# Forgetting attention and FFN on one core: no unread matmuls among the early pairs, the first weight piece behind the first scores, and two FFN quanta fewer beside each of the pairs 8 to 11

## The chip, the cores and the metric

The kernel runs on one core of one Trainium2 chip. Five engines work side by side and meet only at semaphores: TensorE (PE in the profile, its weight loads PEld), VectorE (DVE), ScalarE (ACT), GpSimd (POOL) and SyncE (SP), which here issues all the DMAs. The metric is the device time of the whole program in microseconds (us), lower is better. Three runs of the kernel before took 1208.0, 1208.28 and 1208.91 us; the median is 1208.28 us.

## The reference

Batch 8, 8 heads, sequence 576, head width 64. Attention has a decay that comes from the running sum of log f, and its output goes through a two-layer FFN with 4608 tokens, width 512 and inner width 2048, all in float32:

```python
scores = (1/sqrt(D)) * q @ k.T
cum    = cumsum(log(clip(f, 1e-4, 1)))
scores = where(causal, scores + cum[:, None] - cum[None, :], -1e9)
attn   = exp(scores - max) / (sum + 1e-9)
x      = (attn @ v) laid out as tokens x 512
out    = leaky_relu(x @ w_in, 0.01) @ w_out
```

## The kernel before, in words

The program is written in a fixed order and then reordered by a scheduler that knows the dependencies and its own estimate of each duration: an instruction may be placed ahead of others on its engine when its inputs are ready sooner. A step marked `keep_in_program_order` is pinned behind the step traced just before it on the same engine. Each engine then executes its own list strictly in order.

**Start and pairs.** For the first three batches (`NE = 3`) the first 256 query positions are done early and apart from the rest, two heads at a time: 4 pairs a batch, 12 pairs. In each pass of the loop at line 732, `early_load` fetches the next pair's q, k and v, `early_scores` computes the two row blocks of each head (matmuls `sce<-qk`, then `sce<-both`, which adds the decay; on VectorE the reduction at line 323 with the maximum; on ScalarE the exponential at line 327; then the normalisation, for the first four pairs on VectorE at line 336), `weights` prepares FFN weight pieces, `early_values` transposes and multiplies with v for the pair before, and `fill` issues FFN work. `early_scores` also issues `WARM[1]` matmuls on a tile of zeros after each row block of the first `WARM[2]` pairs. Nothing reads their result. `WARM[0]` more of them stand at the very start of the program.

**Weight pieces.** The FFN weights arrive in 16 pieces of 1 MB (`wraw`), fetched into two buffers, so piece n + 2 can be fetched when piece n is no longer read. `load_weight(n)` converts a piece: ScalarE at line 181 writes `wt`, VectorE shifts it at line 185 (pieces 0 to 4) or 187, ScalarE copies the high part at line 192, VectorE makes the low part (lines 194 and 195, or 206 to 211), and for pieces 0 to 4 TensorE sums it (`ws`), read back at line 204. `wt` has one buffer. For piece 0 the steps of lines 181 and 185 are pinned. `WQ` gives the number of pieces converted beside each pair: one for pairs 1 to 8, two for pairs 9 to 12. Before the loop, pieces 0 and 1 are fetched and piece 0 is converted.

**FFN.** Tokens go through in groups of 256. One block of FFN work for a group, 256 of the inner width, consists of four quanta: two of 12 matmuls `h` (128x256 each), then, for the block before, two of 6 matmuls `o` (128x512). Between them ScalarE applies the activation (`g`, line 654), and `gh` and `gl` split it into a rounded part and a remainder (lines 657 and 659; `gl` is made on VectorE beside the pairs and on POOL beside the heads). `fill(n)` adds n to a credit and issues as many quanta as it holds. `FQ` lists the quanta for each of the 12 pairs and for the pass behind them; three groups, 96 quanta, become ready in this part.

**Heads.** Then the other attention work follows, one head after another (64 tasks, batches in the order of `ORDER`): scores, transposes, values. Beside each head FFN quanta are issued: those ready and not used, `have`, are divided by the heads up to the end of the batch plus `SLACK`, an eighth of the share at each call:

```python
have = ready[0] // T * NQ - used[0]
left = min((e + 2 - t for e in ends if e + 1 >= t), default=1)
step = min(have / (left + SLACK), CAPS.get(t, MAXQ)) / 8
```

When the last head is done, the remaining quanta run one after another to the end.

Of the kernel before, what the change touches and what calls it, by code (L numbers as in the profile page):

```python
# [25 lines left out]
NE = 3  # L26
WQ = (1, 1, 1, 1, 1, 1, 1, 1, 2, 2, 2, 2)
ZE = (("z0", "z1", "z2", "z3"), ("e0", "e1", "e2", "e3"))
FQ = (0, 0, 0, 0, 4, 8, 8, 8, 8, 8, 8, 4, 2)
BUFS = dict(s1=2, m1=2, ost=2)  # L30
RAWS = ("ph", "pl")
WARM = (20, 2, 6)
SCALED = 4
SUMMED = 5
NEG = -1.0e30
# [5 lines left out]
def forgetting_attention_ffn(ctx, tc, qT, kT, v4, vr, f, w_in, w_out, out):  # L41
# [77 lines left out]
    def warm(n):  # L119

        ps = psum.tile([P, 512], F32, tag="h", name=f"warm_{len(warmed)}")
        warmed.append(n)
        for _ in range(n):
            matmul(ps, still[:, :P], still, start=True, stop=True)

    warm(WARM[0])
    eye = one.tile([P, P], F32, tag="part0", name="eye")
# [36 lines left out]
    def fetch_weight(n):  # L164
        raw = raws[n] = one.tile([P, 2, 4 * P, 2], I32, tag=RAWS[n % 2], name=f"wraw_{n}")
        for k, src in enumerate(wpieces[n][0]):
            nc.sync.dma_start(raw[:, k].rearrange("p w two -> p (w two)"), src)
# [47 lines left out]
    def weights(n):  # L215
        while len(loaded) < min(n, len(wpieces)):
            load_weight(len(loaded))
# [80 lines left out]
    def early_scores(b, g):  # L298
# [3 lines left out]
        for i in range(2):  # L302
# [14 lines left out]
            for o in range(2):  # L317
# [11 lines left out]
                )  # L329
            if b * HPB // 2 + g < WARM[2]:  # L330
                warm(WARM[1])
        nc.vector.tensor_scalar(sm, sm, 1.0e-9, None, op0=ALU.add)
# [47 lines left out]
    def fix_z():  # L380

        for i in range(NCH):
            z = fixed[f"z{i}"] = one.tile([P, (i + 1) * P], F32, tag=f"z{i}", name=f"fixed_z{i}")
            nc.gpsimd.memset(z if i == 0 else z[:, i * P + REST:], 0.0)
        fixed["vs"] = one.tile([P, 2, NCH, 2 * D], F32R, tag="vs", name="fixed_vs")

    def split(t):


        s, c0, c1 = tasks[t]  # L390
        h = state[t]
        a, n = c0 * P, S
        x = "ab"[t % 2]
        s1 = h["s1"] = one.tile([P, S], F32R, tag="s1", name=f"s1_{t}", bufs=2)
        m1 = h["m1"] = one.tile([P, S], F32R, tag="m1", name=f"m1_{t}", bufs=2)
        s2, m2 = h["s2"], h["m2"] = fixed["s2" + x], fixed["m2" + x]
        raw = h["raw"]
        for y, x in ((s1[:D, a:n], raw[:D, a:n]), (m1[D:, :n], raw[D:, :n])):
            last = nc.scalar.copy(y, x)  # L399
            if t < 2:  # L400
                tc.keep_in_program_order(last)
        for y in (s1, s2):
            nc.sync.dma_start(y[D:, a:n].bitcast(F32), s1[:D, a:n].bitcast(F32))
        nc.sync.dma_start(m1[:D, :n].bitcast(F32), m1[D:, :n].bitcast(F32))
        nc.sync.dma_start(s2[2:4, a:n].bitcast(F32), dec_q[s][:, a:n])
        nc.sync.dma_start(m2[:2, :n].bitcast(F32), dec_k[s][:, :n])
        minus(m2[D:, :n], raw[D:, :n], m1[D:, :n].bitcast(F32))
        minus(s1[:D, a:n], raw[:D, a:n], s1[:D, a:n].bitcast(F32))
# [291 lines left out]
    def fill(n):  # L700

        settle()
        credit[0] += n
        while credit[0] >= 1:
            credit[0] -= 1
            if not next(quanta, None):
                credit[0] = 0
                return
            used[0] += 1
# [18 lines left out]
    early_load(0, 0)  # L728
    for n in range(len(RAWS)):
        fetch_weight(n)  # L730
    weights(1)
    for x, (b, g) in enumerate(steps + [(NE, 0)]):
        if x + 1 < len(steps):
            early_load(*steps[x + 1])
# [15 lines left out]
        if x == len(steps):  # L750
            split(1)
        fill(FQ[x])
    fix_z()
# [72 lines left out]
```

## Time and profile before

| What | Value |
|---|---|
| Median of three runs | 1208.28 us (1208.0 to 1208.91) |
| Profiled execution, its own time | 1209.36 us |
| Span in the profile, first to last instruction | 1207.5 us |
| TensorE busy | 1194.9 us, 99% |
| TensorE weight loads busy | 1068.1 us, 88% |
| VectorE busy | 613.2 us, 51% |
| ScalarE busy | 633.2 us, 52% |
| GpSimd busy | 460.8 us, 38% |
| HBM read and written | 65.32 MB and 18.58 MB |
| First FFN matmul in the chain | 46.65 us |

How to read it. Busy time is an average over stages with different limits. Matmuls are pipelined and their ends are modelled, so a busy TensorE is not one at its peak. The chain of work that ended last is followed back from the last instruction, at each step to what released it. A timeline row gives the start and length in us, the engine and line, the operation, the tile written and the tiles read, the count, and in brackets the idle time before it with what ended it. A row of the table by stretch gives from : to, its length, then busy us (and count) of TensorE, weight loads, VectorE, ScalarE and GpSimd, then the granted TensorE clock, the DMA engines' share and GB/s.

### The profile page before, as it was taken

The numbers are of one execution on the slowest core, as the hardware profiler recorded it, in microseconds if no ns is written. First come the engines' busy times: TensorE is split into PE (matmuls) and PEld (weight loads), VectorE is DVE, ScalarE is ACT, GpSimd is POOL, SyncE is SP. The second block draws the span as 40 slices with busy tenths as digits, with TensorE's granted clock in tenths as the row PEclk, the third lists the DMA queues.
The fourth block names the chain that finished last, engine by engine and source line by source line (L and its number), as shares of the span: only waits on it lengthen the run. The fifth ranks groups of instructions, "written<-read, shape, count | busy, mean of one in ns | idle before, by whom it ended". The sixth has DMA issues, their size and how long they took to land.

```text
span 1207.5 us, 22521 instructions
## 1 busy us (share of the span) xinstructions
PE 1194.9 (99%) x7828; PEld 1068.1 (88%) x7828; DVE 613.2 (51%) x1697; ACT 633.2 (52%) x1622; POOL 460.8 (38%) x473
## 2 busy tenths in 40 slices
PE   9999999999999999999999999999999999999998
PEld 6678888888899999999999999999999999998997
DVE  6888365566655555464544445444443434553221
ACT  5887465666755565555554545455444445552111
POOL 2000255555455445454435354444354543531000
PEclk9999999999999999999999999999999999999999
DMA  6565233334343233323332223232233223311000
GB/s 202 175 204 177 78 99 101 99 111 118 102 137 82 82 99 101 99 72 97 87 96 79 80 66 101 65 100 59 69 85 93 58 71 81 80 58 52 13 18 19
DMA packets 82130, 110.57 MB, mean 92 GB/s; under 512 B 20640, under 2 KB 51728, under 8 KB 82016
## 3 DMA queue, kind: packets, MB, share of 16 engines
q1 hardware_dynamic: 82016, 109.12, 31.2%
q8 instruction: 63, 1.03, 0.4%
q14 instruction: 51, 0.42, 0.1%
HBM read 65.32 MB, written 18.58 MB: 69 GB/s over the span
## 4 chain that ended last, share of the span: by engine, by line
PE 95%; DVE 2%; ACT 1%; DMA 1%; issue 1%; POOL 0%; SPq 0%; DVEq 0%; ACTq 0%; POOLq 0%
PE h L111 34%; PE o L111 33%; PE tr L115 8%; PE av L111 8%; PE sc L111 7%; PE sce L111 2%; PE ave L111 1%; PE ws L111 1%; PE warm L111 1%; PE tre L115 1%; DVE fixed_z L437 1%; DMA wraw<-in_w_in 0%; ACT g L654 0%; DVE pl L489 0%; DVE gh L657 0%
## 5 line engine op out<-in xcount | busy, mean ns | idle before, releaser
L659 POOL TENSOR_TENSOR gl<-g,gh 128x512 fp32r<-128x512 f32 x113 | 148.8, 1317 | 275.1 <-DVE gh L657 270.1
L111 PE MATMUL o<-wout_h,gh 128*128 128x512 f32 x576 | 231.3, 402 | 0.0
L111 PE MATMUL o<-wout_l,gh 128*128 128x512 f32 x576 | 227.4, 395 | 0.0
L111 PE MATMUL o<-wout_h,gl 128*128 128x512 f32 x576 | 227.1, 395 | 0.0
L443 ACT ACTIVATE fixed_z<-fixed_z,max 128x192 f32<-128x192 f32 (+3 forms) x272 | 161.0, 592 | 101.4 <-DVE max L437 99.1
L111 PE MATMUL h<-xh,win_h 128*128 128x256 f32 x1152 | 206.2, 286 | 0.0
L487 ACT CAST ph<-tr 128x192 fp32r<-128x192 f32 (+3 forms) x360 | 126.7, 373 | 148.5 <-PE tr L115 99.2
L111 PE MATMUL h<-xh,win_l 128*128 128x256 f32 x1152 | 200.3, 283 | 0.0
L437 DVE CUSTOM_DVE_ANT_0 fixed_z<-sc,tri 128x192 f32<-128x192 f32 (+3 forms) x272 | 122.4, 451 | 151.3 <-PE sc L111 148.4
L654 ACT ACTIVATE g<-h 128x512 f32<-128x512 f32 x144 | 85.8, 596 | 216.1 <-PE h L111 211.0
L657 DVE CAST gh<-g 128x512 fp32r<-128x512 f32 x144 | 72.4, 503 | 217.6 <-ACT g L654 215.9
L489 DVE TENSOR_TENSOR pl<-tr,ph 128x384 fp32r<-128x384 f32 (+3 forms) x296 | 137.3, 467 | 80.7 <-ACT ph L487 79.5
L111 PEld LDWEIGHTS h<-xh,win_h 128*128 128x128 f32 x1152 | 170.8, 190 | 5.8 <-issue 0.5
L111 PEld LDWEIGHTS h<-xh,win_l 128*128 128x128 f32 x1152 | 164.8, 190 | 0.5 <-issue 0.2
L111 PE MATMUL h<-xs,win_h 128*128 128x256 f32 x1024 | 164.4, 283 | 0.0
L115 PE MATMUL tr<-ident_r,fixed_z 128*128 128x128 f32 x888 | 145.3, 273 | 3.4 <-DVE ph L494 1.7
L111 PEld LDWEIGHTS h<-xs,win_h 128*128 128x128 f32 x1024 | 141.0, 191 | 0.0
L115 PEld LDWEIGHTS tr<-ident_r,fixed_z 128*128 128x128 f32 x888 | 107.6, 140 | 25.2 <-ACT rb L566 5.2
L111 PEld LDWEIGHTS o<-wout_h,gl 128*128 128x128 f32 x576 | 108.2, 188 | 24.4 <-DVE maxe L323 0.3
L111 PEld LDWEIGHTS o<-wout_l,gh 128*128 128x128 f32 x576 | 108.7, 189 | 16.0 <-issue 0.5
L111 PEld LDWEIGHTS o<-wout_h,gh 128*128 128x128 f32 x576 | 108.9, 189 | 14.8
L154 POOL TENSOR_TENSOR fixed_m2a<-raw,m 64x576 fp32r<-64x576 f32 x32 | 46.6, 1458 | 195.4 <-ACT m L399 173.8
(130 smaller groups left out, 1753.2 us busy)
## 6 DMA issues: line engine op xcount, KB each, us to landing
raw<-in_kT SPq DMA_DIRECT2D x64, 144.0 KB
m<-m SPq DMA_DIRECT2D x64, 144.0 KB
wraw<-in_w_in SPq DMA_DIRECT2D x16, 512.0 KB
wraw<-in_w_out SPq DMA_DIRECT2D x16, 512.0 KB
fixed_vm<-in_v SPq DMA_DIRECT2D x64, 128.0 KB
xs<-xd SPq DMA_DIRECT2D x16, 512.0 KB
out<-ost SPq DMA_DIRECT2D x28, 256.0 KB
raw<-in_qT SPq DMA_DIRECT2D x40, 144.0 KB
```

The source lines that it names most:

```text
L111: nc.tensor.matmul(*args, **kw)
L115: nc.tensor.transpose(*args)
L154: nc.gpsimd.tensor_tensor(out, a, b, op=ALU.subtract)
L437: nc.vector.tensor_tensor_reduce(out=z[:, a:b], in0=ps[:m, :b - a], in1=tri[:m, at:at + b - a], scale=-SCALE, scalar=3.0e38 if x == 0 else ...
L443: nc.scalar.activation(z, z, AF.Exp, bias=h["max"][:m, last:last + 1], scale=-1.0, accum_out=fixed["sum" + "ab"[s // 2 % 2]][:m, i, s % 2: ...
L487: nc.scalar.copy(strided(ph, run), source(ps, run))
L489: nc.vector.tensor_tensor(strided(pl, run), source(ps, run), strided(ph, run).bitcast(F32), op=ALU.subtract)
L654: nc.scalar.activation(g, ph, AF.Prelu, alpha=0.01)
L657: nc.vector.tensor_copy(gh, g)
L659: eng.tensor_tensor(gl, g, gh.bitcast(F32), op=ALU.subtract)
```

## The change

Three constants and one call change. `WARM` keeps the 20 matmuls at the start and drops those among the pairs: after each of two row blocks of six pairs, two each, 24 in all. The call `weights(1)` ahead of the loop goes; piece 0 is then converted by the call `weights(sum(WQ[:x + 1]))` in the loop's first pass, behind `early_scores` of the first pair, and the two pinned steps of piece 0 follow that pair's steps on ScalarE and VectorE. The later passes convert the same pieces as before. In `FQ` the pairs 8 to 11, counted from 1, have 6 quanta each where they had 8; the eight quanta stay ready and are issued by the later calls of `fill`.

```diff
-FQ = (0, 0, 0, 0, 4, 8, 8, 8, 8, 8, 8, 4, 2)
+FQ = (0, 0, 0, 0, 4, 8, 8, 6, 6, 6, 6, 4, 2)
 BUFS = dict(s1=2, m1=2, ost=2)
 RAWS = ("ph", "pl")
-WARM = (20, 2, 6)
+WARM = (20, 0, 0)
...
     early_load(0, 0)
     for n in range(len(RAWS)):
         fetch_weight(n)
-    weights(1)
     for x, (b, g) in enumerate(steps + [(NE, 0)]):
```

## The prediction

> **What bounds the kernel now.** I read the page first: busy shares (its part 1) and the chain that ended last (part 4).
>
> ```profile
> PE 1194.9 (99%) x7828; PEld 1068.1 (88%) x7828; DVE 613.2 (51%) x1697; ACT 633.2 (52%) x1622; POOL 460.8 (38%) x473
> PE 95%; DVE 2%; ACT 1%; DMA 1%; issue 1%; POOL 0%; SPq 0%; DVEq 0%; ACTq 0%; POOLq 0%
> ```
>
> TensorE is busy 99% of the span and carries 95% of the chain. So the time is TensorE's work plus the short stretches in which it lacks work: work taken out counts, but only where nothing else then ends last. The table by stretch (us busy per engine) shows where another engine is close:
>
> ```profile
> 46.00:75.00 29.00, 29.00 (x194) 23.60 (x192) 27.73 (x59) 22.21 (x50) 0.00 (x0) 1.00 0.58 194
> 75.00:83.00 8.00, 8.00 (x49) 5.49 (x47) 5.99 (x18) 6.71 (x18) 0.00 (x0) 1.00 0.63 210
> 83.00:95.00 12.00, 12.00 (x78) 9.60 (x77) 10.58 (x23) 10.23 (x25) 0.00 (x0) 1.00 0.56 181
> 95.00:110.50 15.50, 15.46 (x100) 12.91 (x98) 12.47 (x25) 9.67 (x22) 0.00 (x0) 1.00 0.59 202
> 110.50:127.50 17.00, 16.20 (x99) 13.05 (x98) 11.84 (x24) 11.59 (x25) 3.06 (x2) 1.00 0.38 117
> ...
> 160.00:200.00 40.00, 39.16 (x263) 35.36 (x263) 23.99 (x63) 23.10 (x60) 23.25 (x26) 1.00 0.35 96
> 200.00:250.00 50.00, 49.40 (x335) 44.97 (x334) 28.69 (x91) 34.22 (x89) 24.42 (x27) 1.00 0.40 106
> 250.00:300.00 50.00, 47.99 (x324) 43.09 (x323) 30.91 (x97) 33.49 (x94) 28.10 (x30) 1.00 0.39 109
> 300.00:350.00 50.00, 48.81 (x329) 44.13 (x327) 31.36 (x94) 32.22 (x91) 24.13 (x24) 1.00 0.42 117
> 350.00:400.00 50.00, 50.00 (x340) 45.59 (x339) 27.86 (x81) 28.98 (x81) 26.62 (x26) 1.00 0.34 98
> ```
>
> The third busy number is VectorE. Beside the pairs it is nearly full (27.73 of 29.00 us from 46 to 75), and from 83 on it has 12% to 30% left. From 160 to 350 TensorE sits idle for 0.84 + 0.60 + 2.01 + 1.19 = 4.64 us, from 350 to 400 not at all. These are the two places that the moved FFN work leaves and enters.
>
> **Part 1: 24 matmuls go.** The first argument of `WARM` stays, so 20 of the 44 remain.
>
> ```profile
> L111 PE MATMUL warm<-still x44: 388/393/792, 1.5 to 56.2; 128*128 128x512 f32 x44
> ```
>
> ```profile
> 8.80 4.30 PE warm L111 x18
> ...
> 13.28 0.51 PE warm L111 x2
> ...
> 46.65 2.02 PE h L111 x17
> ...
> 54.61 0.47 PE warm L111 x2
> ...
> 56.15 0.47 PE warm L111 x2
> ```
>
> The chain charges 4.30 + 0.51 = 4.81 us to the 20 that were drawn ahead into the first scores, and 0.94 us to the other four. If TensorE had other work ready everywhere, the sum would be -5.75 us. It has not. The four at 54 to 57 stand where VectorE is 96% busy (27.73 of 29.00), so their ends are 0 and -0.94; I take -0.5, the middle, as both engines are near full there.
>
> For the 20, timeline rows (start, length) tell what stands behind them:
>
> ```profile
> 7.84 0.79 DVE L230 TENSOR_TENSOR both<-d,both 64x128 fp32r<-64x128 f32 x2
> ...
> 8.73 4.38 PE L111 MATMUL warm<-still 128*128 128x512 f32 x18
> 9.96 1.13 ACT L181 ACTIVATE wt<-wraw 128x1024 f32<-128x1024 f32 x1 [1.77 <-DMA wraw<-in_w_in]
> ...
> 12.95 0.34 PE L111 MATMUL sce<-both 128*128 128x128 f32 x2
> ...
> 13.32 0.29 DVE L323 CUSTOM_DVE_ANT_0 ze<-sce,tri 128x128 f32<-128x128 f32 x1 [4.68 <-PE sce L111]
> ...
> 13.71 0.40 ACT L327 ACTIVATE ze<-ze,maxe 128x128 f32<-128x128 f32 x1 [2.63 <-DVE maxe L323]
> ...
> 13.73 0.85 PE L111 MATMUL sce<-qk 64*128 64x256 f32 x4
> ...
> 13.75 0.69 DVE L185 TENSOR_SCALAR wt<-wt 128x1024 int32<-128x1024 int32 x1
> ...
> 15.20 1.23 DVE L195 SCALAR_TENSOR_TENSOR win_l<-wraw 128x1024 fp32r<-128x1024 uint32 x1
> ...
> 16.45 0.81 SPq L167 DMA_DIRECT2D wraw<-in_w_in  x2
> ...
> 18.28 0.41 DVE L323 CUSTOM_DVE_ANT_0 ze<-sce,tri 128x256 f32<-128x256 f32 x1
> ...
> 21.09 1.00 DVE L336 TENSOR_SCALAR ze<-ze,sume 128x128 f32<-128x128 f32 x4
> ```
>
> The decay rows `both` are ready at 7.84 + 0.79 = 8.63, but the matmul that adds them to the scores starts at 12.95, behind 18 unread matmuls; VectorE idles 4.68 us for it, and ScalarE 2.63 us. Without them that matmul follows at 8.73: everything of pair 0 begins 12.95 - 8.73 = 4.22 us earlier.
>
> **Part 2: piece 0 behind pair 0's scores.** The move issues no DMA and shifts no fetch: both fetches stay ahead of it in SP's queue. What moves is its first ScalarE step (L181), pinned behind the step traced before it, now the last exponential of pair 0; and its first VectorE step (L185), pinned behind the last of pair 0's four scalings (L336). So I lay out pair 0 from the rows: first reductions at 13.32 - 4.22 = 9.10, second score matmuls at 13.73 - 4.22 = 9.51 for 0.85, adding the decay for about 0.4, the wider reductions (0.41 each) at about 10.7 and 11.1, two exponentials to about 12.2, sum and reciprocal 0.35, scalings 1.00: end at about 13.5. L185 then starts at about 13.5 where it started at 13.75: piece 0 gains almost nothing (the low bound, 0.25 us), pair 0 the full 4.2 (the other bound). Between them: VectorE's stretch from 13.75 to 21.09 + 1.00 = 22.09 holds the two wide reductions (0.82), two small steps (0.35) and the scalings (1.00), about 2.2 us, that now lie ahead of piece 0; what remains ends 2.2 + 0.25, about 2.5 us, earlier. That value lies nearest to VectorE's rows, which are what ended the waits there, so I take -2.5 us of the 4.81; the other 2.3 us TensorE waits for piece 0 and the exponentials.
>
> Behind the late L181 and L185 stand the rest of piece 0 and the fetch of piece 2 (16.45, when L195 ends and its buffer is free). That fetch stays where it was and is what is late next:
>
> ```profile
> 18.00:20.00 2.00, 1.24 (x6) 0.93 (x7) 1.99 (x9) 1.89 (x7) 0.00 (x0) 1.00 0.96 389
> 20.00:21.00 1.00, 1.00 (x3) 0.25 (x3) 0.83 (x5) 1.00 (x3) 0.00 (x0) 1.00 0.42 168
> 21.00:22.00 1.00, 1.00 (x8) 0.66 (x8) 1.00 (x5) 0.55 (x4) 0.00 (x0) 1.00 0.00 0
> ```
>
> ```profile
> 23.53 1.14 ACT L181 ACTIVATE wt<-wraw 128x1024 f32<-128x1024 f32 x1
> ```
>
> The last two columns are the DMA engines' share and GB/s: they move nothing from 21 to 22, and ScalarE reads piece 2 at 23.53: at least 2.5 us of cover, just enough for the 2.5 us taken.
>
> **Part 3: eight quanta leave pairs 8 to 11.** Two columns of 12 `h` matmuls and two of 6 `o` matmuls make a block of four quanta; the chain's last full block:
>
> ```profile
> 1192.64 2.77 PE o L111 x12
> 1195.42 2.87 PE h L111 x24
> ```
>
> So a quantum is (2.77 + 2.87) / 4 = 1.41 us, eight are 11.3 us. This work is not saved: it must be done later, and it is free only where the pairs' stretch gets shorter by as much. From 75 to 127.5 us that leaves TensorE 52.5 - 11.3 = 41.2 us. VectorE has 5.99 + 10.58 + 12.47 + 11.84 = 40.9 us there, less two blocks' `gh` and `gl`:
>
> ```profile
> 100.09 0.43 DVE gh L657
> ...
> 101.64 0.68 DVE gl L659
> ```
>
> 2 x 1.11 = 2.2, so 38.7 us. At the 96% of the row 46 to 75 this takes 40.3 us and costs nothing; at the 88% of 83 to 95, 43.9 us, +2.7; at the 80% of 95 to 110.5, 48.1 us, +6.9. With less TensorE work beside it VectorE will wait less, so the value lies between the first two: +1.5 us. The quanta come back beside the first attention heads (96 ready quanta less the 58 used before, now 50, so 46 in place of 38; a head takes 9 calls of an eighth of that over 12, its remaining heads and slack: 8 / 12 x 9 / 8 = 0.75 more a head). The idle 4.64 us there is the most that this can win, nothing the least; I take a third, -1.5 us, since those waits come in links of the heads' own chain, not all of them where a quantum is put. `gl` of the two blocks passes to POOL, 38% busy.
>
> **Sum.** -2.5 - 0.5 + 1.5 - 1.5 = -3.0 us. The profiled execution took 1209.36 us (1.86 outside its span), 1.08 above the median of the three runs; against it 1206.4, against the median of 1208.28 it is 1205.3 us. A change under 0.2%, 2.4 us, can't be told from none here.
>
> **Rivals.**
> 1. *All of the 20 matmuls' time is won, and the stalls beside the heads too*: -4.2 - 0.9 + 0 - 3 = -8.1, 1200.2. For it: pair 0 does start 4.2 earlier. Against: piece 0 doesn't.
> 2. *The 20 were cover only*: piece 0, not pair 0, leads the start; -0.25 - 0.5, no net effect of the quanta: 1207.5, no change. For it: L185 moves 13.75 to 13.5 only. Against: VectorE has 4.68 us idle ahead of it.
> 3. *The pairs' stretch is held by the weight pieces*, VectorE at the 80% of 95 to 110.5: the eight quanta leave, the stretch shrinks by 4.4 and not 11.3. Then +6.9 in place of +1.5: +2.4, 1210.7, slower. It decides where VectorE's share falls below about 85% (38.7 / 0.85 = 45.5 us, +4.3, which eats up all the rest). For it: 110.5 to 127.5 shows 70%. Against: there TensorE, with eight quanta, was the one full.
> 4. *TensorE's clock drops in the thin start.* Matmul counts per 2 us show that the chip starts slow:
>
> ```profile
> 2.00:4.00 2.00, 2.00 (x6) 1.57 (x5) 1.00 0.77 223
> ...
> 6.00:8.00 2.00, 2.00 (x11) 1.61 (x9) 1.00 1.01 373
> ```
>
> Six unread matmuls before 4 us, eleven after 6, though the granted-clock column says 1.00 in both. From 8.73 to about 13.5 TensorE would have only about 2 of 4.8 us filled. If it went back to the slow rate until refilled, about 4.5 us (the slow stretch at the start) to 9 us of its work would take 11/6 as long: +4 to +7; with +4, 1209.3, no change. The Trainium skill, "TensorE: Matmul & The Clock Gate", Part 1, says that the clock falls after an idle window of about 3.4 us and rises after a busy one as long. The trace agrees with the rise; no gap that I lay out reaches an idle window, so by that rule the rival doesn't happen.
>
> **Chances.** The forecast 0.48, rival 1 0.12, rival 2 0.17, rival 3 0.13, rival 4 0.10. The forecast's own spread is about 3 us to either side: an eighth of it falls under 0.2%. Faster: 0.42 + 0.12 and 0.04 from rivals 2 and 4; slower: rival 3 and 0.02 of rival 4; the rest the same. The range goes from near rival 1 to rival 3: 1200.5 to 1210.5; the likeliest case alone is 1202.3 to 1208.3.
>
> **What would show it.** Right: 20 unread matmuls left; the decay matmul of pair 0 at about 8.8 and L185 at 13 to 14; the first `h` matmul, at 46.65 before, 2 to 3 us earlier; the pairs' end some 13 us earlier, the last full blocks at the old pace; less TensorE idle from 150 to 340. Wrong: piece 2's first step waiting for its DMA; TensorE idle beside pairs 8 to 11 with ScalarE waiting for a weight piece; matmul spacing near twice the old one between 10 and 20 us; the heads' idle time unchanged although each has more to fill it with.

## The result and the profile after

The changed kernel took 1216.27 us (median of five runs, 1215.22 to 1218.69), the kernel before, run beside it, 1208.28 (1207.43 to 1208.91): a ratio of 1.0070, interval 1.0055 to 1.0085. It is 8.0 us slower; the forecast was 3 us faster. The profiled execution took 1215.97 us, with a span of 1214.2. Among the runs below, two executions far out of line with the others of their kernel, 1910.39 us of the first experiment and 4068.62 us of the changed kernel with the old quanta, are left out of medians and ranges.

The page of the changed kernel, busy time and the chain by engine:

```profile
PE 1197.7 (99%) x7804; PEld 1067.9 (88%) x7804; DVE 620.2 (51%) x1696; ACT 632.6 (52%) x1622; POOL 461.9 (38%) x474
PE 92%; DVE 2%; ACT 2%; DMA 1%; issue 1%; POOL 1%; SPq 1%; ACTq 0%; POOLq 0%; DVEq 0%
```

TensorE runs 24 matmuls fewer and is busy 2.8 us longer, with 92% of the chain in place of 95%. Both point at a short stretch in which the chain leaves TensorE and its matmuls get longer. The chain of the first 60 us (start, length) shows where it leaves:

```profile
6.93 6.91 DMA qk<-in_kT
13.97 6.33 PE sce L111 x14
...
21.91 4.12 PE ws L111 x6
```

Until 13.84 the transfer of pair 1's k ends last, then scores are computed, and piece 0's products (`ws`) come only behind them. The timeline of the start (start, length, engine, line, count, and in brackets the idle time before with what ended it):

```profile
8.38 0.44 PE L111 MATMUL sce<-both 128*128 128x128 f32 x2
...
8.86 0.29 DVE L323 CUSTOM_DVE_ANT_0 ze<-sce,tri 128x128 f32<-128x128 f32 x1 [0.22 <-PE sce L111]
...
12.00 1.09 ACT L181 ACTIVATE wt<-wraw 128x1024 f32<-128x1024 f32 x1
...
13.97 0.76 PE L111 MATMUL sce<-qk 64*128 64x128 f32 x2 [3.41 <-DMA qk<-in_kT]
...
15.17 0.29 DVE L323 CUSTOM_DVE_ANT_0 ze<-sce,tri 128x128 f32<-128x128 f32 x1 [3.92 <-PE sce L111]
...
18.31 1.00 DVE L336 TENSOR_SCALAR ze<-ze,sume 128x128 f32<-128x128 f32 x4
...
19.22 0.69 DVE L185 TENSOR_SCALAR wt<-wt 128x1024 int32<-128x1024 int32 x1
```

Pair 0 starts as early as forecast. But between its last reduction and its scalings VectorE's list now holds reductions of pair 1 (at 15.17, after 3.92 us of waiting), and TensorE's list has all of pair 1's scores ahead of piece 0. Those scores wait 3.41 us for k, which was requested behind the 2 MB of the first two weight pieces. Piece 0's shift (L185) starts at 19.22, where it started at 13.75 before.

The table by stretch (from : to, length, busy us of TensorE, weight loads, VectorE, ScalarE and GpSimd, granted clock, DMA share, GB/s) shows the second thing:

```profile
0.00:10.00 10.00, 8.16 (x30) 6.12 (x30) 5.83 (x15) 5.07 (x11) 6.14 (x19) 1.00 0.70 220
10.00:20.00 10.00, 6.59 (x17) 3.93 (x16) 3.68 (x18) 3.81 (x13) 0.00 (x0) 0.60 0.39 137
20.00:30.00 10.00, 10.00 (x36) 5.60 (x36) 6.08 (x19) 4.75 (x10) 0.00 (x0) 0.71 0.27 88
```

A granted clock of 0.60 and 0.71 over 10 us each is (0.40 + 0.29) x 10 / 0.5 = 13.8 us at half clock. The trace's record of the clock has it as one stretch from 12.07 to 25.72, 13.65 us, which is four times 3.41 us, the shortest fall in these traces before the last 4 us of the program; 3.41 us at half clock is called a window below. The kernel before had 1.00 here throughout. All five runs of the changed kernel had a mean clock of 0.993 or 0.994; the 15 to 23 runs of before that stood beside each group of experiments nearly all had 1.0.

The heads, which were to take the eight moved quanta for nothing, give back nothing that their idle time shows:

```profile
160.00:200.00 40.00, 39.91 (x269) 36.26 (x268) 21.58 (x59) 21.45 (x56) 22.88 (x25) 1.00 0.33 91
200.00:250.00 50.00, 49.94 (x336) 45.03 (x335) 28.88 (x88) 30.36 (x83) 24.50 (x26) 1.00 0.39 111
250.00:300.00 50.00, 46.79 (x323) 42.67 (x324) 33.13 (x95) 33.78 (x95) 25.46 (x25) 1.00 0.38 108
300.00:350.00 50.00, 48.46 (x326) 43.81 (x325) 31.08 (x98) 34.36 (x95) 24.03 (x26) 1.00 0.39 107
```

TensorE is idle 0.09 + 0.06 + 3.21 + 1.54 = 4.90 us from 160 to 350, where it was 4.64. The small gaps before 250 are gone; a single one of 2.5 us at 270 has taken their place.

### The profile page after: what moved, and what is told of

It reads as the page before. It is cut to its first block, busy times and chain, and to the rows that moved or that the text cites. A ratio compares the mean times of both kernels' runs of the same rounds, so it can differ in the third digit from the quotient of the medians.

```text
span 1214.2 us, 22471 instructions
## 1 busy us (share of the span) xinstructions
PE 1197.7 (99%) x7804; PEld 1067.9 (88%) x7804; DVE 620.2 (51%) x1696; ACT 632.6 (52%) x1622; POOL 461.9 (38%) x474
## 4 chain that ended last, share of the span: by engine, by line
PE 92%; DVE 2%; ACT 2%; DMA 1%; issue 1%; POOL 1%; SPq 1%; ACTq 0%; POOLq 0%; DVEq 0%
PE h L111 33%; PE o L111 32%; PE tr L115 8%; PE av L111 8%; PE sc L111 7%; PE sce L111 2%; PE ws L111 1%; PE ave L111 1%; PE tre L115 1%; DMA qk<-in_kT 1%; DVE fixed_z L437 0%; DMA wraw<-in_w_out 0%; DVE pl L489 0%; DVE wraw L207 0%; DMA fixed_s2a<-s 0%
## 5 line engine op out<-in xcount | busy, mean ns | idle before, releaser
L659 POOL TENSOR_TENSOR gl<-g,gh 128x512 fp32r<-128x512 f32 x114 | 152.0, 1333 | 283.7 <-DVE gh L657 280.1
L657 DVE CAST gh<-g 128x512 fp32r<-128x512 f32 x144 | 75.4, 524 | 205.5 <-ACT g L654 204.1
L111 PE MATMUL sc<-m,s 128*128 128x288 f32 (+1 forms) x336 | 121.2, 365 | 0.5 <-DVE max L437 0.4
```

Source lines behind the costliest of these rows:

```text
L111: nc.tensor.matmul(*args, **kw)
L657: nc.vector.tensor_copy(gh, g)
L659: eng.tensor_tensor(gl, g, gh.bitcast(F32), op=ALU.subtract)
```

## The experiments

Times are medians; ratios are to the kernel before, run on the same chip. "Mean clock" is the granted clock over one execution. The first theory, A, was that pair 1's late transfer makes the gap and the gap drops the clock; B, that the thin start drops it with or without the gap; C, that the quanta cost.

### One part at a time

**Pair 1 fetched ahead of the weight pieces** (changed kernel; the lists of TensorE and VectorE stay):

```diff
     early_load(0, 0)
+    early_load(*steps[1])
     for n in range(len(RAWS)):
...
-        if x + 1 < len(steps):
+        if 1 < x + 1 < len(steps):
             early_load(*steps[x + 1])
```

> The changed kernel with pair 1's q, k and v fetched ahead of the two weight pieces; the order of TensorE's and VectorE's lists is that of the changed kernel. Theory A (pair 1's scores stand ahead of piece 0 in both lists and wait until 13.97 us for a transfer queued behind 2 MB of weights; the 3.4 us gap then halves TensorE's clock): the gap at 10.6 to 14.0 goes, L185 starts at 14 to 15 us and not at 19.22, the clock doesn't fall, and the kernel takes 1203 to 1207 us. Theory B (the start without unread matmuls is too thin for the clock, whatever is waited for): the clock still falls for some 10 us, 1211 us or more. Theory C (the eight FFN quanta are what costs): 1215 us or more, since they stay moved.

1214.01 us (1211.74 to 1215.14), ratio 1.0044, 1.0031 to 1.0057. The gap is gone and the shift starts at 15.6 instead of 19.2. The clock fell all the same:

```profile
10.00:14.00 4.00, 3.53 (x15) 2.25 (x15) 1.85 (x13) 3.03 (x10) 0.00 (x0) 0.99 0.95 366
14.00:20.00 6.00, 6.00 (x16) 3.67 (x16) 4.68 (x15) 3.61 (x11) 0.00 (x0) 0.50 0.25 67
```

TensorE's rows cover 3.53 of the 4 us before the fall, all of them small score matmuls, and the clock halves behind them. So A's second half fails: the gap is not needed. It costs more with the gap (four windows in place of two, from 13.90 on), but B is the better account of the clock in this run. C, 1215 or more, fell.

**The order alone** (kernel before without the call `weights(1)`; the 24 unread matmuls and the old quanta stay):

> The kernel before with piece 0 behind pair 0's scores alone; the 24 unread matmuls and the FFN quanta stay as before. Theory A: the unread matmuls cover the wait for pair 1, so the clock stays at 1.0, but piece 0 is still behind pair 1's scores in the lists, L185 starts at 17 to 19 us and the kernel takes 1210 to 1213 us. Theory B: with the unread matmuls in place nothing is lost, 1207 to 1209 us. Theory C: 1207 to 1209 us.

1215.51 us (1212.34 to 1215.96), ratio 1.0049, 1.0036 to 1.0061. Moving the call alone makes most of the loss; B and C, which had 1207 to 1209, fell. Two of its five executions had a clock of 1.0, and they took 1212.34 and 1212.76, in A's range: 3.5 to 4.0 us of loss with no fall of the clock at all. In the other three the clock fell although the unread matmuls were in place, which A did not have. In the profiled one it fell for two windows from 17.65 on, with no gap over 0.41 us in the 4 us before it, and the shift started at 20.3.

**The unread matmuls alone** (kernel before with `WARM = (20, 0, 0)`):

> The kernel before without the 24 unread matmuls among the pairs alone; piece 0 stays ahead of the loop, the quanta as before. Theory A: piece 0 is ahead of pair 1 in both lists, so no gap of 3 us; L185 at 11.2 to 12 us, clock at 1.0, 1203 to 1206 us. Theory B: the thin start lets the clock fall, 1209 to 1214 us. Theory C: as theory A.

1209.23 us (1206.99 to 1211.72, eleven runs), ratio 1.0006, 0.9998 to 1.0015. The three executions at clock 1.0 took 1206.99 to 1208.56, those below, 1208.22 to 1211.72. The shift starts at 10.6. A's 1203 to 1206 was missed; the median and the lower clocks are B's. At full clock the three lie 0.3 to 1.8 us under the median of before, whose own runs go from 1207.27 to 1210.34, so that a gain is not shown; in most executions the clock takes it back in any case.

**The quanta alone** (kernel before with the new `FQ`):

> The kernel before with the eight FFN quanta moved alone. Theories A and B: what the pairs' stretch loses the heads give back, 1206 to 1210 us. Theory C: 1213 us or more.

1212.89 us (1208.51 to 1214.70, ten runs), ratio 1.0029, 1.0018 to 1.0040. The two executions at clock 1.0 took 1208.51 and 1208.63, as before and as A and B had it. The others lost about 4, and the median lies between the ranges of A and B (to 1210) and of C (from 1213). The chain near the last weight pieces:

```profile
111.76 0.45 SPq L296
...
112.30 0.55 SPq L360
...
112.90 0.42 SPq L167
...
113.38 6.61 DMA wraw<-in_w_out
```

With less FFN work beside it the last weight fetch (L167) is reached behind other transfers in SP's queue, and ScalarE's step waits until 120.09. TensorE idles 2.34 us at 120.5, and the clock falls for a window:

```profile
120.00:127.00 7.00, 4.66 (x22) 3.14 (x21) 4.31 (x12) 4.60 (x11) 2.50 (x5) 0.76 0.12 34
```

### Filling the gap, nothing else

To part the clock from the order, unread matmuls were put into TensorE's finished list at one place, ahead of pair 1's first score, so that every useful instruction keeps its place in the list:

```python
HELD = [(14, 'sce_0_1_0', 0)]
...
        spare = unread[3:3 + sum(n for n, *_ in HELD)]
...
        for n, tile, k in HELD:
...
            made[at:at] = spare[:n]
```

`n` is how many, and they go ahead of the k-th matmul into this tile; they are made as extra ones at the start of the program (`WARM` is `(34, 0, 0)`) and taken out there.

> The changed kernel with 14 more unread matmuls (0.23 us each, 3.2 us together) in TensorE's list right before pair 1's first score matmul, where it stood idle from 10.56 to 13.97 us; the order of all other instructions of TensorE is the changed kernel's own. Nothing useful becomes earlier, so only the clock can move the time. Theory G (the idle 3.4 us drop the clock from 12.07 to 25.72): clock 1.0 throughout, about 1209 to 1211, that is after less 6 to 7. Theory S (a stretch that holds nothing but 64-row score matmuls also counts as thin): no fall at 12, but one or two windows at half clock between 14 and 22, mean clock 0.995 to 0.998, 1211 to 1214. Theory Q (only the place of piece 0 costs, the clock is no part of it): as the changed kernel, 1215 to 1218.

1212.96 us (1210.76 to 1214.93), ratio 1.0035, 1.0022 to 1.0049. In its trace the clock is 1.00 from 10 to 26: fourteen matmuls that compute nothing win 3.3 us. Theory G had the clock right; S, that scores alone must drop it, missed here on the clock, though its range holds the median, and Q fell. The one execution at 1.0 (1210.76) lay in G's range, the median did not: in the profiled execution the clock fell later, at 267, behind the 2.5 us gap in the heads. This run and the first experiment don't fit one rule: there the clock fell behind scores with no gap over 0.41 us, here it held through 3.7 us of them.

With eight more among pair 1's scores:

> As the run before (14 unread matmuls in the gap), and 2 more before each of four score matmuls of pairs 1 and 2 (8, at most 1.84 us on the path to piece 0). Theory G: no more than before is won, 1209 to 1212.5, clock 1.0 in both. Theory S: here alone the clock holds, 1.0, and the time is 1209 to 1212, under the run before by 1 to 3. Theory Q: 1216 to 1219.

1213.08 us (1212.05 to 1214.31), ratio 1.0035, 1.0023 to 1.0048; clocks 0.998 to 1.0. Nothing more is won, as G has it, though the median lies above G's range (1209 to 1212.5); S, by which the time falls here, missed.

The changed kernel with the old quanta, without and with the gap filled:

> The changed kernel with the quanta of before (8 beside each of pairs 7 to 10 in the list's count). If the quanta are about neutral once the start has been lost: 1214.5 to 1218, the changed kernel's time within 1.5. If the quanta cost about 4 as they did alone on the kernel before: 1211 to 1213.

1218.07 us (1217.52 to 1218.85), ratio 1.0077, 1.0063 to 1.0090. That is just above the range of the first case, quanta about neutral (to 1218); that they cost about 4, the second, fell.

> The changed kernel with the 14 unread matmuls in the gap, and the quanta of before. With the gap filled and the new quanta it took 1212.96, and 1210.76 in the run whose clock was 1.0; its trace has one idle stretch of 2.50 us at 265 (and one window of half clock behind it), where kernels with the old quanta have none over 0.9 in the heads. Theory H (the new quanta cost nothing at full clock, but leave that stretch, and with it a window of half clock in most runs, 1 to 2 us): 1210 to 1212, clocks 0.999 to 1.0. Theory C (the new quanta cost the pairs' stretch about 1.3 and the heads give nothing back): 1209 to 1210 at clock 1.0. Rival (they gain, as the two runs without the gap filled suggest, 1216.27 with them and 1218.07 without): 1212.5 to 1215.

1212.98 us (1211.31 to 1213.63), ratio 1.0037, 1.0024 to 1.0049, with a clock of 1.0 in all five executions. H and C missed; the range of the rival, that the new quanta gain, holds the time. The medians with new and old quanta are equal (1212.96 and 1212.98), but the clock isn't: the one execution of the new quanta at 1.0 took 1210.76, the five of the old 1211.31 to 1213.63, so that a gain of the new quanta at full clock isn't excluded. Here the stretch in the heads is gone, the clock holds, and the kernel is still 4.4 us slower. So the clock is worth 5.1 us here (1218.07 to 1212.98), and 4.4 us of the loss of this version have another cause.

### What costs at full clock: piece 0's place

The traces point at the chain of weight pieces. First and last start of the shift of pieces 0 to 4 on VectorE (L185), before, after, and with the gap filled and old quanta:

```profile
L185 DVE TENSOR_SCALAR wt<-wt x5: 687/687/690, 13.7 to 40.1; 128x1024 int32<-128x1024 int32 x5
```

```profile
L185 DVE TENSOR_SCALAR wt<-wt x5: 686/690/694, 19.2 to 50.0; 128x1024 int32<-128x1024 int32 x5
```

```profile
L185 DVE TENSOR_SCALAR wt<-wt x5: 685/686/694, 17.4 to 44.6; 128x1024 int32<-128x1024 int32 x5
```

The fifth piece is 9.9 us late in the changed kernel and 4.5 us late where the clock holds. VectorE's read of the products (L204) had no idle time before it from 20 to 65 us before the change. With the gap filled it has, in each of five pieces, and so has the changed kernel (first row: gap filled, second: changed kernel; us and times):

```profile
  PE ws L111: 5.2, 5
```

```profile
  PE ws L111: 7.7, 5
```

In the new lists each piece's products stand behind scores on TensorE, while VectorE's read of them stands ahead of other work on VectorE; VectorE waits there five times. Its busy time from 20 to 65 us (third number) is 39.78 us before, 32.35 in the changed kernel and 34.29 with the gap filled:

```profile
20.00:65.00 45.00, 44.95 (x250) 31.00 (x251) 39.78 (x111) 35.24 (x84) 0.00 (x0) 1.00 0.55 184
```

```profile
20.00:65.00 45.00, 44.99 (x208) 27.74 (x207) 32.35 (x87) 31.37 (x72) 0.00 (x0) 0.94 0.49 167
```

```profile
20.00:65.00 45.00, 44.98 (x231) 29.62 (x230) 34.29 (x90) 31.82 (x74) 0.00 (x0) 1.00 0.51 169
```

The test is to move piece 0 alone. Changed kernel with the call between the two halves of pair 0's scores:

```diff
         for i in range(2):
             ...
+            if (b, g, i) == (0, 0, 0):
+                weights(1)
```

> The changed kernel with one call moved: piece 0's conversion is called between the two halves of pair 0's scores instead of behind all of them, so that in VectorE's list it stands ahead of pair 0's scaling and of pair 1 (which waits for its transfer until about 14 us), and piece 0's products stand ahead of pair 1's scores in TensorE's. Theory P (the time follows the chain of weight pieces, one us for one us: the fifth piece's shift on VectorE starts at 40.1 in the kernel before, at 50.0 in the changed one at +8, at 44.6 with the gap filled and the old quanta at +4.4, at 38.0 without unread matmuls at -1.6 in its run at full clock): the first shift at 10 to 11, the fifth at 37 to 40, 1206 to 1209, a window of half clock in the start adding 1 to 3 where it falls before the fifth piece. Theory K (what costs is only the missing cover for the clock, wherever piece 0 stands): half clock for two to four windows, 1213 to 1216.

1208.24 us (1205.09 to 1210.13, twelve runs), ratio 0.9996, 0.9987 to 1.0004. One moved call wins back all 8 us, with the 24 unread matmuls still gone and the quanta still new. P's range holds the time, and K falls. The shifts run from 12.2 (P had 10 to 11) to 37.3, the wait of L204 is 0.6 us once, and VectorE's busy time is mostly back:

```profile
L185 DVE TENSOR_SCALAR wt<-wt x5: 683/687/693, 12.2 to 37.3; 128x1024 int32<-128x1024 int32 x5
```

```profile
20.00:65.00 45.00, 44.86 (x252) 30.70 (x251) 37.45 (x106) 34.06 (x81) 0.00 (x0) 1.00 0.55 174
```

TensorE had a gap of 1.36 us in this start, at 11.64, and in the profiled execution the clock did not fall there; it did for one window at 263.6, behind the 2.51 us gap in the heads.

So piece 0's place is what costs. That the loss is one us for each us of the fifth piece, as P had it, the single traces don't bear out: P set the lateness of a trace beside the median of all executions. Taking the time of the traced execution itself, less the median of before, the fifth shift is 9.9 us late and the execution 7.7 us longer in the changed kernel; the pairs of numbers are 9.9 and 6.8 with the call alone moved, 9.6 and 8.9 with the old quanta, 5.6 and 2.9 with pair 1 fetched first, 4.3 and 4.1 with the gap filled, and 4.5 and 2.7 with that and the old quanta. That is 0.5 to 0.95 us for each late us, falls of the clock included. And moving the call also takes the wait for k from in front of piece 0, so that the chain of pieces is not tested apart from it.

Taking away the pins of piece 0's steps instead moves it further up, ahead of pair 0's decay matmuls:

> The changed kernel without the two pins that hold piece 0's first conversion steps in the program's order: the planner then puts piece 0 ahead of pair 0's first reductions on VectorE and its products ahead of pair 0's decay matmuls on TensorE. Theory P: first shift under 10, fifth at 34 to 38, 1203 to 1207. Rival (the pairs, not the pieces, set the stretch once the pieces are early; pair 0 and 1 come 2 to 4 later than in the changed kernel): 1207 to 1211.

1215.78 us (1211.94 to 1217.32), ratio 1.0052, 1.0040 to 1.0064. A miss for P and for its rival. The fifth shift is early, at 39.5, but TensorE idles 3.78 us ahead of piece 0's first product and 3.98 us at 122, and the clock fell three times (0.994 in the profiled execution).

> As the run before, with the quanta of before. If the quanta are about neutral (gap filled: 1212.96 and 1212.98): within 1 of the run before, by Theory P 1203 to 1207, and clocks nearer 1.0, since the heads have no idle stretch of 2.5 us. If the new quanta gain at full clock: 1 to 2 above it.

1209.44 us (1208.05 to 1210.50, eleven runs), ratio 1.0005, 0.9997 to 1.0014. Not within 1 us of the run before, and later than P's range: the fifth shift starts at 37.6, and nothing is won by it. The gap at 122 is not there with the old quanta, the one at the start is 1.98 us and not 3.78, and none of the three falls is there; together that makes 6 us here. So P holds for lateness only, and not one for one: a piece chain behind that of before goes with a loss, one ahead of it (37.0 to 38.6 us in the traces of seven versions of this document) wins 1.3 us at most in the medians.

### Holding the clock without the 24 matmuls

Seven extra unread ones put in the idle places of the kernel that lacks the 24 (the extra ones at the start shifted the planner's order a little):

> The kernel before without its 24 unread matmuls among the pairs (as the run with that alone), but with 7 left: 3 right before piece 0's first product, 2 between its products and 2 before pair 1's first score, where that run's trace shows TensorE idle for 0.84, 0.40 and 0.41 us; TensorE's order of the first pairs shifts a little. If the unread matmuls among the pairs cost about 2 us of path and are worth their place only as a hold on the clock: clock 1.0 in nearly all runs and 1206 to 1208. If 7 don't hold it: as the run without any, 1207 to 1212 with clocks of 0.997 to 1.0. If they were free: 1208 to 1209.5.

1209.42 us (1208.32 to 1213.13, eleven runs), ratio 1.0011, 1.0002 to 1.0020. The clock holds (0.999 or 1.0 in every execution), and the time is no better: its lead over the trace of before, 3.6 us in a reduction at 96, is 0.2 us in the first reduction of the heads at 146. The median lies in the range of the third case, that the unread matmuls were free; what they cost of path is not shown by this pair of runs.

Five of the 20 at the start moved there, so that the order stays:

> The kernel before without its 24 unread matmuls among the pairs, every useful instruction in the order of that run; of the 20 unread ones at the start 5 are moved: 3 ahead of piece 0's first product and 2 ahead of its third, into idle time of 0.84 and 0.40 us. If that run's lower clocks (0.997 to 0.999 in 8 of 11 executions) came from windows there: clock 1.0 in nearly all, 1206.5 to 1208.5. If they fell elsewhere: as that run, 1207 to 1211. If fewer unread ones at the very start let the clock start late: 1209 to 1213.

1209.39 us (1207.69 to 1212.28, eleven runs), ratio 1.0005, 0.9996 to 1.0014; clocks 0.995 to 1.0. The first case missed; the ranges of the two others both hold the median. With 15 at the start TensorE runs dry at 6.98 for 1.21 us and at 10.62 for 1.46, and the profiled execution has three windows of half clock before 25 us.

> The kernel before without its 24 unread matmuls, once more, for a trace of an execution with another phase: 1207 to 1212; where its clock is under 1.0, the window of half clock lies in the start (10 to 20 us) if thin stretches there drop it, or beside the last weight pieces (100 to 130) or in the heads (250 to 310).

1207.77 us, clock 0.999. The same program that held 1.0 in its first trace fell in this one, behind a gap of 1.70 us at 10.00:

```profile
10.00:14.00 4.00, 2.30 (x5) 0.90 (x5) 2.62 (x3) 2.72 (x6) 0.00 (x0) 0.78 0.77 275
```

### The quanta, with piece 0 first

Three runs change `FQ` alone on that kernel; the numbers are those beside pairs 8 to 12.

Old (8, 8, 8, 8, 4):

> The changed kernel with piece 0's call between the halves of pair 0's scores, and the quanta of before. With the new quanta it took 1208.24 (clock 0.997 to 0.999 in every execution), and its trace is 3.9 us ahead of the kernel before until 260 and loses 3.0 of that between 260 and 267, in an idle stretch of 2.51 us and one window of half clock behind it. Theory H (that stretch is the new quanta's): here no idle stretch over 0.9 in the heads, clocks nearer 1.0, and 1205 to 1207. If the pairs' stretch loses with the old quanta what the heads win: 1207.5 to 1209.5.

1209.94 us (1206.18 to 1211.92, eleven runs), ratio 1.0008, 0.9999 to 1.0017. The stretch at 260 is gone as forecast, but H's time was missed, and the median lies just above the range of the other case. A gap of 1.98 us stands at 110; the one fall of this trace lies elsewhere, at 11.76, in a gap of 1.58 us.

Seven each (7, 7, 7, 7, 4):

> Piece 0 between the halves of pair 0's scores as before, with 7 quanta beside each of pairs 8 to 11 (6 gave 1208.24, 8 gave 1209.94). If what the quanta decide is only which idle stretches appear (2.51 us at 260 with 6, 1.98 us at 110 with 8, each with the chance of a window at half clock): neither stretch here, clocks 0.999 to 1.0, 1205.5 to 1207.5, faster than both kernels. If a stretch of 2 us or more turns up in another place: 1208 to 1210.

1211.30 us (1209.02 to 1214.85, eleven runs), ratio 1.0019, 1.0010 to 1.0029: later than both cases had it. The trace has a stretch of 2.59 us at 161 with a window behind it, and two more windows at 11.65 and 111.

Late (6, 6, 6, 8, 6):

> As that run, with 6, 6, 6, 8 quanta beside pairs 8 to 11 and 6 beside pair 12 (54 in all, as with seven each). Same theories: 1205.5 to 1207.5 without an idle stretch of 2 us in the heads or beside the last pieces, 1208 to 1210 with one.

1207.54 us (1205.17 to 1208.61, eleven runs), ratio 0.9988, 0.9979 to 0.9998. Just above the range of the first case (to 1207.5). No gap over 1.36 us anywhere, and the heads fill (150 to 350 us: with 6, 6, 6, 6, 4, then this one):

```profile
150.00:350.00 200.00, 195.10 (x1307) 176.97 (x1307) 121.33 (x348) 123.75 (x336) 103.38 (x106) 0.99 0.38 106
```

```profile
150.00:350.00 200.00, 197.03 (x1323) 177.33 (x1322) 120.59 (x363) 128.75 (x351) 105.15 (x109) 1.00 0.39 108
```

This version is faster than the changed kernel beyond doubt, and than the kernel before by 0.12%, at the edge of what can be told, the more so as it is the best of four tried. The number of quanta does not order the four (1208.24, 1209.94, 1211.30, 1207.54); the longest idle stretch (2.51, 1.98, 2.59, 1.36 us) does so better: the shortest goes with the fastest and the longest with the slowest, and the intervals of the two between overlap. That is four traces of one execution each, and 2.51 and 2.59 us go with 1208.24 and 1211.30; a cause is not shown by it.

## Why the prediction was wrong

**Part 2 failed, and the loss comes from it.** Its layout of pair 0 was right: decay matmul at 8.73, measured 8.38; first reduction 9.10, measured 8.86; wide reductions 10.7 and 11.1, measured 10.48 and 10.83; last exponential 12.2, and L181 follows at 12.00. Then it let the sum, the scalings and L185 follow at 13.5, because the pin names only pair 0's steps. L185 started at 19.22. The step that failed is "its first VectorE step (L185), pinned behind the last of pair 0's four scalings (L336)", read as *right behind*. The pin says what must come before, not what may not; pair 1's work, unpinned, was put between. It then waited for a k that was requested behind 2 MB. In the trace of before the transfer was issued at the same place (k at 6.48, after at 6.93), but its reader started at 18.76 and waited for VectorE, so that no row of waits named it; the order of SP's queue did. "That fetch stays where it was", said of piece 2, fell with it: 16.45 became 22.32. The term of the sum, -2.5 us, has the wrong sign: the move alone costs 3.5 to 4.0 us at full clock and 6.7 in the median.

**The price of a late piece** was not in the sum. Rival 3 named the weight pieces, but for the stretch from 75 us on and through VectorE's share. The late first five pieces go with a loss of 3.5 to 4.0 us at full clock with the call alone moved, and of 4.4 with the gap filled and the old quanta; that piece 0's place costs it is shown by the moved call, that it does so through the chain of pieces is argued from VectorE's waits.

**Rival 4 happened, at about its price.** It was priced at +4 to +7 us, and filling the gap wins 3.3 to 5.1. It got 0.10, since no gap that was laid out reached an idle window. The gap that came had 3.41 us. But the reason given would have failed too: the clock fell in the first experiment behind a stretch in which TensorE's rows covered 3.53 of 4 us, and elsewhere behind gaps of 1.70 and 2.34 us. The Trainium skill, "TensorE: Matmul & The Clock Gate", Part 1, ties the fall to an idle window of about 3.4 us; the traces here show falls with much less idle time than that. It also says that the window is free-running. With that the traces agree: one program held 1.0 in one execution and lost a window in the next. Together, clock and late pieces make the 8: filling the gap wins 3.3 us with the new quanta, and what is left is 4.4 us (1212.96 against 1208.58). Of these a part is still clock, which fell in the heads: the one execution at 1.0 was 2.2 us behind. So the split between the two is known to 2 us only.

**Part 1** was priced too high: -2.5 (together with part 2) and -0.5 were taken, and without the 24 matmuls the ratio of 1.0006 is +0.7 us (interval -0.2 to +1.8), in three executions at full clock -0.3 to -1.8. What the sum lacked is what the matmuls do for the clock: without them it was below 1.0 in 8 of 11 executions, with them (the kernel before, beside it) in 1 of 22.

**Part 3.** The sum of +1.5 and -1.5 came out near zero where the clock held: 1208.51 and 1208.63 with the quanta alone. The terms were too small: 11.3 - 1.5 = 9.8 us of the stretch should go, and the last reduction of pair 12 starts 8.0 us earlier with the new quanta when the gap is filled (135.7 to 127.7), 8.8 when it isn't (141.8 to 133.0), and only 5.3 with the quanta alone (130.6 to 125.3). So the stretch keeps 2.5 to 6.0 us. What was not in the sum is the stall that the moved work opens elsewhere, at 120 (the last fetch) or 265, by what else is in the kernel: at clock 1.0 the quanta alone cost nothing, in the other eight executions about 4 us.

Of the signs listed: the 20 unread matmuls and the early decay matmul were right. L185 was off by 5 us. Five `h` matmuls came far earlier, the first at 29.76, but the twelfth starts at 55.02 in place of 47.80. The last reduction of pair 12 came 2.4 us later (133.0, 130.6 before) where the pairs' end was to come some 13 us earlier. Two of the four signs for "wrong" came: the half clock between 10 and 20 us and the heads' idle time. A third, the wait for a weight piece beside the pairs, came with the quanta alone, at 120, and not in the changed kernel. Piece 2's first step waited for no transfer.

## What to carry to other kernels

A pin or a dependency bounds an instruction from one side only: before pricing a move, write down what the planner may put between, and for each such instruction when its own input lands, its place in the DMA queue included. Price a late step by the chain behind it (here each late us of the piece chain went with 0.5 to 0.95 us of the kernel) and not by the idle time of the engine that it sits on; an early one wins far less. Matmuls that compute nothing can be worth more than their time where TensorE would stand idle (fourteen of them won 3.3 us here), and a quantum of work moved out of a stretch should be followed to the queue that it was covering.

## What was not expected of the hardware

The granted clock halves for whole windows of some 3.4 us (3.41, 6.83 and 13.65 us in these traces), and whether it does so differs between executions of one program: 0.997 to 1.0 over eleven executions of the kernel without unread matmuls, which at 1.0 took 1206.99 to 1208.56 us and else up to 1211.72. Gaps of 1.70, 2.34 and 2.51 us were followed by such a window, and one of 1.36 us at the start was in one trace (seven quanta) and was not in two others. The same gap does not always do it: one of 2.50 or 2.51 us between 260 and 273 stands in seven traces, and the clock fell at it in three (gap filled, piece 0 between the halves, no pins) and held in four (the changed kernel, pair 1 fetched first, the quanta alone, gap and scores filled). What share of a window must be idle, and whether the small score matmuls count less than their rows show, was not settled: in the first two experiments the clock fell behind thin stretches with no gap over 0.41 us in the 4 us before, and in two others (the gap filled, with new and old quanta) it held through 3.7 us of scores without a gap.
